# Eight unread products in place of seven in front of the first attention scores of a fused kernel

## The chip, the cores and the metric

The kernel runs on one core of a Trainium2 chip. The metric is device microseconds of one execution. The engines are TensorE (PE; PEld is its weight load), VectorE (DVE), ScalarE (ACT), GpSimd (POOL) and SyncE (SP, which here only issues transfers).

## The reference

Three blocks follow each other on 2 x 768 rows: an attention whose scores are a window of keys plus 24 block summaries (maxima of the keys, means of the values), a gated feed-forward block, and a mixer over rows and channels. Cut to what matters:

```
k_sum = k.reshape(B, H, nb, 32, D).max(axis=3)
v_sum = v.reshape(B, H, nb, 32, D).mean(axis=3)
scores = [where(|i - j| < 16, q @ k.T / 8, -1e9), q @ k_sum.T / 8 + log(32)]
x  = softmax(scores) @ [v, v_sum]
xk = mu_k * x + (1 - mu_k) * x_prev          # x_prev: the row before
xr = mu_r * x + (1 - mu_r) * x_prev
x  = sigmoid(xr @ w_r) * (relu(xk @ w_k) ** 2 @ w_v)
u  = x + (relu(x.T @ w_tok1) @ w_tok2).T
return u + relu(u @ w_ch1) @ w_ch2
```

The weights come as 64-bit floats.

## The kernel before

Attention works on tiles of 128 rows. For the first of the two batches a step is one tile and every second head (`e` 0 or 1); for the second batch both halves go together. In a step, `s_stage` makes 8 or 16 small score products (sp, L367) into one of two score banks per half; VectorE masks and reduces them (L385, four per half), ScalarE takes exponentials (L387), the second batch is normalised on GpSimd (L399), TensorE transposes (pt, L405), a copy brings the result back (PT, L408 or L410), and `v_stage` multiplies with the values (pv, L425). In the first batch `rb` (L441) spreads the normalisers and L445 applies them. The block maxima are ks (L287, VectorE), which GpSimd copies into each key tile (kw, L293, twelve copies per batch: the "key sums" below); the block means are vrs (L309), transposed into vp (L318), copied to vs (L320, ScalarE) and spread by small transfers (L339).

Work of the feed-forward block fills the gaps: `main` multiplies with w_k (ko, L541), squares (`k2_tile`: rl L553 on ScalarE and L554 on VectorE, kh L555 on ScalarE, kl L556 on GpSimd) and multiplies with w_v (acc, L541). Its input is mixed in `mixed` (tmp L530 on GpSimd, xk L531 on VectorE, xh L532, xl L533). Each operand is held as a rounded high part and a low part, so one product is three. A weight block is decoded in `Weights.step`: L153 on ScalarE, L157 and L163 on VectorE into one of two wf buffers, then the high part by L174 on ScalarE and the low part by L175 on GpSimd; L157 of the next but one weight waits until that L175 has freed its buffer. A float32 product is two passes and so two records in the trace; a product of the rounded type is one.

`spin(n)` issues n products of the unit matrix with itself (128 x 512) into the bank of ko. Nobody reads them. `SPIN0` of them stand in front of everything else on TensorE, and one more behind each of the first `SPIN_UNITS` attention steps.

The order on each engine is not written by hand. The program is recorded in the order of the Python code, and a scheduler with a timeline of its own then places the instructions of each engine; `ahead(n)` gives a call a higher priority, `behind` and `after` add an order without a wait on the chip. An instruction of another length early in the program can therefore move others far from it.

Of the kernel before, what the change touches and what calls it, by code (L numbers as in the profile page):

```python
# [28 lines left out]
RATIO, NR, RATIO2 = 1.2, 25, 1.8  # L29
SIDE_EVERY = 3  # L30
AHEAD = 4
SPIN0 = 7
SPIN, SPIN_UNITS = 1, 8
WFIRST = 2
S2COST, S3COST, S4COST = 4, 2, 3
# [22 lines left out]
def fused_kernel(ctx, tc, q, k, v, vt, mu, w_k, w_v, w_r, w_t1, w_t2, w_c1, w_c2, out):  # L58
# [557 lines left out]
    def spin(n):  # L616

        o = bank("ko", 1, [128, 4, 128], "spin")
        for _ in range(n):
            after(nc.tensor.matmul(o, ident, ident.unsqueeze(1).to_broadcast([128, 4, 128]), start=True, stop=True))  # L620


    spin(SPIN0)
    for t in range(NT):
# [515 lines left out]
```

## Time and profile before

| | us |
|---|---|
| three runs | 506.04, 506.87, 511.75 (median 506.87) |
| profiled execution | 506.84 |
| its span, first to last instruction | 504.9 |
| around the span | 1.94 |
| TensorE busy | 489.1 (97%) |
| VectorE, ScalarE, GpSimd busy | 319.6, 239.7, 240.0 |

Times in the trace count from the span's start. The busy time of TensorE is that of products as they follow each other; it tells that TensorE had work, not that it ran at its peak. PEclk is the granted clock as a share of the full 2.4 GHz; 0.50 is the other level, 1.2 GHz.

### The profile page before, as it was taken

What the parts mean: (1) busy time and instruction counts of PE and PEld (TensorE: products, weight loads), DVE (VectorE), ACT (ScalarE), POOL (GpSimd) and SP (SyncE); (2) the same over time, 40 slices, a digit from 0 to 9 for tenths busy, and PEclk for the clock granted to TensorE, in tenths of its full rate; (3) what the DMA queues carried; (4) which work ended last, traced back from release to release, by engine and by line L of the source; (5) the groups of instructions that cost most, each with busy time, mean ns of one, the idle gap of its engine ahead of it and who ended that gap; (6) DMA issues with size and microseconds to landing.
All of it is one profiled execution on the core that took longest, in us unless ns stands there. A gap on an engine that the chain in (4) does not pass through costs nothing.

```text
span 504.9 us, 8793 instructions
## 1 busy us (share of the span) xinstructions
PE 489.1 (97%) x3278; PEld 407.0 (81%) x3278; DVE 319.6 (63%) x638; ACT 239.7 (47%) x541; POOL 240.0 (48%) x294
## 2 busy tenths in 40 slices
PE   7999997999999999999999999999999999999996
PEld 3567785888888898887887787878888999989995
DVE  3888998641514365698789789646479638354352
ACT  1778746872443545655456555554554435011110
POOL 5335587862543457488845535764941813000000
PEclk9899998899999999999999999999999999999999
DMA  8999940321000650000550999629351404163102
GB/s 265 298 294 345 345 124 13 89 80 40 20 1 1 233 186 0 1 0 7 162 167 5 386 398 329 215 91 320 132 167 42 140 30 167 51 201 112 56 1 83
DMA packets 35914, 70.63 MB, mean 140 GB/s; under 512 B 3072, under 2 KB 12288, under 8 KB 35872
## 3 DMA queue, kind: packets, MB, share of 16 engines
q1 hardware_dynamic: 34288, 69.09, 42.1%
q10 hardware_dynamic: 1584, 0.98, 0.7%
q8 instruction: 26, 0.43, 0.4%
q14 instruction: 16, 0.13, 0.1%
HBM read 60.04 MB, written 9.44 MB: 138 GB/s over the span
## 4 chain that ended last, share of the span: by engine, by line
PE 65%; DVE 14%; DMA 11%; ACT 4%; POOL 3%; issue 3%; SPq 1%; DVEq 0%; ACTq 0%; POOLq 0%
PE o L952 12%; PE ko L541 11%; PE m L541 11%; PE acc L541 10%; PE o L980 7%; PE go L541 5%; DMA wst<-in_moe_w_v_dram 4%; PE ro L541 3%; DVE wf L163 3%; DMA wst<-in_moe_w_ch_dram 2%; DMA xT<-in_vt_dram 2%; DVE xk L531 2%; PE pv L425 2%; PE sp L367 2%; DVE xl L533 2%
## 5 line engine op out<-in xcount | busy, mean ns | idle before, releaser
L175 POOL TENSOR_TENSOR w<-wf,w 128x512 fp32r<-128x512 f32 x50 | 69.0, 1387 | 60.8 <-ACT w L174 57.7
L541 PE MATMUL ko<-xh,w 128*128 128x256 f32 x384 | 76.4, 288 | 1.7 <-POOL w L175 0.9
L541 PE MATMUL m<-u,w 128*128 128x256 f32 x504 | 65.1, 283 | 0.7 <-DVE mw L843 0.7
L541 PEld LDWEIGHTS m<-u,w 128*128 128x128 f32 x504 | 63.4, 191 | 2.8 <-DVE mw L843 0.9
L541 PEld LDWEIGHTS ko<-xh,w 128*128 128x128 f32 x384 | 61.2, 188 | 5.4 <-POOL w L175 1.1
L541 PE MATMUL acc<-w,kh 128*128 128x512 f32 x192 | 61.4, 404 | 0.0
L952 PE MATMUL o<-w,gh 128*128 128x512 f32 x192 | 59.1, 391 | 0.0
L541 PE MATMUL ko<-xl,w 128*128 128x256 f32 x192 | 54.4, 283 | 1.1 <-DVE xl L533 1.1
L174 ACT CAST w<-wf 128x512 fp32r<-128x512 f32 x50 | 30.9, 620 | 50.3 <-DVE wf L163 48.5
L163 DVE SCALAR_TENSOR_TENSOR wf<-wst,wf 128x512 int32<-128x512 int32 x50 | 47.5, 958 | 8.8 <-ACT wst L153 7.7
L556 POOL TENSOR_TENSOR kl<-rl,kh 128x512 fp32r<-128x512 f32 x24 | 34.3, 1430 | 36.0 <-ACT kh L555 32.6
L530 POOL TENSOR_SCALAR tmp<-xT,oms 128x256 f32<-128x256 f32 x52 | 38.5, 748 | 21.2 <-DVE xk L531 12.4
L554 DVE TENSOR_TENSOR rl<-rl 128x512 f32<-128x512 f32 x24 | 18.7, 781 | 46.0 <-ACT rl L553 45.8
L387 ACT ACTIVATE pe<-pe,mn 128x120 f32<-128x120 f32 x96 | 36.6, 383 | 14.8 <-DVE mn L385 14.6
L531 DVE SCALAR_TENSOR_TENSOR xk<-xT,mus,tmp 128x256 f32<-128x256 f32 x52 | 39.3, 788 | 5.1 <-POOL tmp L530 4.7
L153 ACT ACTIVATE wst<-wst 128x512 f32<-128x512 f32 x62 | 40.9, 674 | 2.7 <-DMA wst<-in_moe_w_ch_dram 2.7
L541 PEld LDWEIGHTS acc<-w,kh 128*128 128x128 f32 x192 | 35.3, 192 | 7.3 <-ACT pe L387 0.3
L952 PEld LDWEIGHTS o<-w,gh 128*128 128x128 f32 x192 | 34.7, 188 | 6.2
L541 PE MATMUL acc<-w,kl 128*128 128x512 f32 x96 | 37.8, 404 | 0.9 <-POOL kl L556 0.9
L541 PEld LDWEIGHTS ko<-xl,w 128*128 128x128 f32 x192 | 36.2, 188 | 2.2 <-DVE xl L533 1.3
L952 PE MATMUL o<-w,gl 128*128 128x512 f32 x96 | 37.1, 391 | 0.0
L541 PE MATMUL go<-u,w 128*128 128x512 f32 x144 | 35.7, 393 | 0.0
(119 smaller groups left out, 950.9 us busy)
## 6 DMA issues: line engine op xcount, KB each, us to landing
wst<-in_moe_w_ch_dram SPq DMA_DIRECT2D x36, 512.0 KB, 7.3
w<-stored SPq DMA_DIRECT2D x24, 512.0 KB, 5.5
stored<-w SPq DMA_DIRECT2D x24, 256.0 KB, 4.8
wst<-in_moe_w_k_dram SPq DMA_DIRECT2D x8, 512.0 KB, 7.9
wst<-in_moe_w_v_dram SPq DMA_DIRECT2D x8, 512.0 KB, 9.9
wst<-in_moe_w_tok_dram SPq DMA_DIRECT2D x6, 512.0 KB, 4.9
out_dram<-o SPq DMA_DIRECT2D x12, 256.0 KB, 2.3
kw<-in_k_dram SPq DMA_DIRECT2D x9, 320.0 KB, 5.0
```

Source lines behind the costliest of these rows:

```text
L153: a = nc.scalar.activation(top.bitcast(F32), top.bitcast(F32), AF.Prelu, scale=2.0 ** -112, alpha=2.0 ** 32)
L163: nc.vector.scalar_tensor_tensor(wi, top, 3, wi, ALU.logical_shift_left, ALU.bitwise_or)
L174: r = nc.scalar.copy(hi, src)
L175: eng.tensor_tensor(lo, src, hi.bitcast(F32), ALU.subtract)
L387: nc.scalar.activation(pe, pe, AF.Exp, bias=mn[:, p:p + 1], scale=-1.0, accum_out=den[:, p:p + 1])
L530: nc.gpsimd.tensor_scalar(tmp, xT[:, d, x0 - 1:x0 - 1 + MW], om[:, d:d + 1], 1.0, ALU.mult, ALU.mult)
L531: nc.vector.scalar_tensor_tensor(xk[:, d], xT[:, d, x0:x0 + MW], mu[:, d:d + 1], tmp, ALU.mult, ALU.add)
L541: nc.tensor.matmul(o, l, r, start=(first and i == 0), stop=(last and i == 3 * n - 1))
L554: nc.vector.tensor_tensor(rl, rl, rl, ALU.mult)
L556: nc.gpsimd.tensor_tensor(lo, rl, hi.bitcast(F32), ALU.subtract)
L952: nc.tensor.matmul(accs[c][t], l, r, start=(first and j == 0 and i == 0), stop=(last and j == 1 and i == 2))
L980: nc.tensor.matmul(accs[0][t], l, r, start=(k == 0 and i == 0), stop=(k == NF2 - 1 and i == 2))
```

## The change

One constant: the number of products that stand in front of everything else on TensorE.

```
-SPIN0 = 7
+SPIN0 = 8
```

All else follows from the scheduler. The set of instructions is the same but for that product. On TensorE the order differs at two places, between the 73rd and the 95th product and between the 337th and the 561st, of 2834; on VectorE, ScalarE and GpSimd in the same stretches of time, and on SyncE in two query loads (L353) that go behind transfers of vs (L339). After that all engines stand as before.

The start of TensorE, as the difference of the two programs (spin are the unread products, sp the scores):

```order
 L1136 UNCONDITIONAL_BRANCH
-L620 MATMUL spin<-ident 128x512 x7
+L620 MATMUL spin<-ident 128x512 x8
 L367 MATMUL sp<-kw,xT 64x120 x13
 L620 MATMUL spin<-ident 128x512
```

Only the count moved here. VectorE while the key maxima of the second batch are made (ks), before:

```order
L287 TENSOR_REDUCE ks<-kw 128x4x4
L531 SCALAR_TENSOR_TENSOR xk<-xT,mus,tmp 128x256
L163 SCALAR_TENSOR_TENSOR wf<-wst,wf 128x512
L445 TENSOR_TENSOR xT<-xT,rb 128x4x128
L157 TENSOR_SCALAR wf<-wst 128x512
L287 TENSOR_REDUCE ks<-kw 128x4x4
L531 SCALAR_TENSOR_TENSOR xk<-xT,mus,tmp 128x256
L554 TENSOR_TENSOR rl<-rl 128x512
L163 SCALAR_TENSOR_TENSOR wf<-wst,wf 128x512
L309 TENSOR_REDUCE vrs<-ybuf 128x48
L157 TENSOR_SCALAR wf<-wst 128x512
L287 TENSOR_REDUCE ks<-kw 128x4x4 x2
```

and now:

```order
L157 TENSOR_SCALAR wf<-wst 128x512
L287 TENSOR_REDUCE ks<-kw 128x4x4
L157 TENSOR_SCALAR wf<-wst 128x512
L445 TENSOR_TENSOR xT<-xT,rb 128x4x128
L531 SCALAR_TENSOR_TENSOR xk<-xT,mus,tmp 128x256
L163 SCALAR_TENSOR_TENSOR wf<-wst,wf 128x512
L531 SCALAR_TENSOR_TENSOR xk<-xT,mus,tmp 128x256
L163 SCALAR_TENSOR_TENSOR wf<-wst,wf 128x512
L554 TENSOR_TENSOR rl<-rl 128x512
L309 TENSOR_REDUCE vrs<-ybuf 128x48
L287 TENSOR_REDUCE ks<-kw 128x4x4 x2
L157 TENSOR_SCALAR wf<-wst 128x512
```

One weight step (L157) went from ahead of the last two maxima to behind them, and the other L157 and the fourth maximum came up ahead of L445. TensorE around the last scores of the second batch's first pair, before (acc and ko are products of the feed-forward block, vp transposes of the block means):

```order
L541 MATMUL ko<-xh,w 128x256
L541 MATMUL acc<-w,kl 128x512
L541 MATMUL acc<-w,kh 128x512 x2
L541 MATMUL acc<-w,kl 128x512
L318 MATMUL vp<-ident,vrs 24x128 x2
L367 MATMUL sp<-kw,qT 64x120
L541 MATMUL ko<-xh,w 128x256
L541 MATMUL ko<-xl,w 128x256
```

and now:

```order
L318 MATMUL vp<-ident,vrs 24x128 x2
L541 MATMUL acc<-w,kl 128x512 x2
L541 MATMUL acc<-w,kh 128x512 x2
L541 MATMUL acc<-w,kl 128x512
L541 MATMUL acc<-w,kh 128x512 x2
L541 MATMUL acc<-w,kl 128x512
L367 MATMUL sp<-kw,qT 64x120 x4
L541 MATMUL ko<-xh,w 128x256
L541 MATMUL ko<-xl,w 128x256
L367 MATMUL sp<-kw,qT 64x120 x3
L541 MATMUL ko<-xh,w 128x256 x2
```

The acc group that stood ahead of the single last score stands ahead of seven scores now, and the ko products behind or between them. ScalarE at the same place, before (rl empties the bank of ko, the CAST makes a weight's high part, pe are exponentials):

```order
L174 CAST w<-wf 128x512
L153 ACTIVATE wst<-wst 128x512
L553 ACTIVATE rl<-ko 128x512
L174 CAST w<-wf 128x512
L153 ACTIVATE wst<-wst 128x512
L320 ACTIVATE vs<-vp 24x512
L555 CAST kh<-rl 128x512
L387 ACTIVATE pe,den<-pe,mn 128x120 x8
```

and now:

```order
L320 ACTIVATE vs<-vp 24x512
L174 CAST w<-wf 128x512
L153 ACTIVATE wst<-wst 128x512
L387 ACTIVATE pe,den<-pe,mn 128x120 x2
L174 CAST w<-wf 128x512
L553 ACTIVATE rl<-ko 128x512
L153 ACTIVATE wst<-wst 128x512
L387 ACTIVATE pe,den<-pe,mn 128x120 x6
L555 CAST kh<-rl 128x512
```

L553, which stood ahead of a weight's cast, stands behind it and behind two exponentials; L555 (kh) stands behind six more.

## Rows read from the trace of the kernel before

**Rows 1.** The page, part 1: TensorE, busy us, share of the span, instructions.

```profile
PE 489.1 (97%) x3278; PEld 407.0 (81%) x3278; DVE 319.6 (63%) x638; ACT 239.7 (47%) x541; POOL 240.0 (48%) x294
```

**Rows 2.** Busy us (count) by engine in four stretches, then PEclk, DMA share, GB/s.

```profile
40.00:60.00 20.00, 17.93 (x234) 15.12 (x228) 20.00 (x61) 15.72 (x50) 12.97 (x14) 1.00 1.06 360
80.00:92.00 12.00, 8.94 (x56) 6.64 (x57) 11.24 (x47) 8.86 (x35) 9.03 (x12) 0.72 0.22 59
92.00:110.00 18.00, 17.94 (x218) 15.05 (x216) 8.09 (x47) 15.08 (x53) 13.78 (x30) 1.00 0.24 66
110.00:501.00 391.00, 388.01 (x2315) 332.25 (x2313) 235.40 (x364) 167.71 (x310) 173.87 (x162) 1.00 0.36 121
```

**Rows 3.** The chain of waits: start us, us, what.

```profile
36.73 7.66 DMA wst<-in_moe_w_k_dram
```

**Rows 4.** TensorE in order of time, 79 to 92 us (idle before, releaser in brackets).

```profile
79.45 0.41 PE L367 MATMUL sp<-kw,qT 64*64 64x120 f32 x2
80.63 0.39 PE L541 MATMUL ko<-xh,w 128*128 128x256 f32 x1 [0.77 <-ACT rl L553]
...
82.04 0.50 PE L541 MATMUL ko<-xh,w 128*128 128x256 f32 x2 [0.91 <-POOL w L175]
...
85.01 0.63 PE L367 MATMUL sp<-kw,qT 64*64 64x120 f32 x2 [1.52 <-issue]
...
87.57 1.87 PE L367 MATMUL sp<-kw,qT 64*64 64x120 f32 x30
...
91.89 0.40 PE L541 MATMUL acc<-w,kl 128*128 128x512 f32 x1
92.12 0.28 PE L541 MATMUL ko<-xh,w 128*128 128x256 f32 x1
```

**Rows 5.** TensorE in two stretches: length, busy us, PEclk, DMA share, GB/s.

```profile
12.70:15.95 3.25, 3.25 (x23) 0.50 1.06 322
84.30:91.05 6.75, 6.04 (x40) 0.50 0.27 62
```

**Rows 6.** TensorE products and weight loads in order of time, the first 12 us.

```profile
1.46 8.41 PE L620 MATMUL spin<-ident 128*128 128x512 f32 x14 [1.46 <-POOL ident masks.py:199]
...
8.85 0.19 PEld L620 LDWEIGHTS spin<-ident 128*128 128x128 f32 x1 [0.24 <-issue]
...
11.94 1.78 PE L367 MATMUL sp<-kw,xT 64*64 64x120 f32 x26 [2.08 <-POOL kw L293]
```

**Rows 7.** VectorE in order of time, weight steps.

```profile
58.95 1.29 DVE L157 TENSOR_SCALAR wf<-wst 128x512 int32<-128x512 int32 x1
...
66.98 0.48 DVE L157 TENSOR_SCALAR wf<-wst 128x512 int32<-128x512 int32 x1
...
80.78 1.75 DVE L163 SCALAR_TENSOR_TENSOR wf<-wst,wf 128x512 int32<-128x512 int32 x1
```

**Rows 8.** GpSimd in order of time, 68 to 91 us.

```profile
68.74 4.85 POOL L293 TENSOR_SCALAR kw<-ks 128x96 f32<-128x96 f32 x12
73.57 1.26 POOL L556 TENSOR_TENSOR kl<-rl,kh 128x512 fp32r<-128x512 f32 x1
...
79.63 0.96 POOL L530 TENSOR_SCALAR tmp<-xT,oms 128x256 f32<-128x256 f32 x2 [1.86 <-DVE xT L445]
80.56 1.43 POOL L175 TENSOR_TENSOR w<-wf,w 128x512 fp32r<-128x512 f32 x1
...
89.44 1.39 POOL L399 TENSOR_SCALAR pe<-pe,den 128x120 f32<-128x120 f32 x4 [2.61 <-DVE den L396]
```

**Rows 9.** ScalarE in order of time, one exponential.

```profile
85.05 0.38 ACT L387 ACTIVATE pe<-pe,mn 128x120 f32<-128x120 f32 x1
```

**Rows 10.** The queue of SyncE, in order of time.

```profile
84.27 4.87 SPq L339 DMA_DIRECT2D vw<-vs  x5
```

**Rows 11.** VectorE and GpSimd in order of time, 51 to 53 us.

```profile
51.23 0.68 DVE L163 SCALAR_TENSOR_TENSOR wf<-wst,wf 128x512 int32<-128x512 int32 x1
51.39 1.65 POOL L175 TENSOR_TENSOR w<-wf,w 128x512 fp32r<-128x512 f32 x1 [3.98 <-ACT w L174]
```

## Prediction

> **What bounds the kernel now.** I read the page's slices first, then busy time by stage, then the chain of waits of the first 140 us, then each engine in order of time from 56 to 102 us. TensorE carries the span: 489.1 of 504.9 us [rows 1], and from 110 us to its last product at 501 us it stands still for 3.0 us in all (391 less 388.01) [rows 2]. What is won or lost before 110 us therefore reaches the end nearly one for one, because the order of the products after that point is the same in both kernels. Before that two other things rule. Up to about 44 us the chain runs through transfers, weight after weight; its last piece lands at 44.39 [rows 3]. From 40 to 60 us VectorE is busy for 20.00 of 20 us [rows 2]. Between 80 and 92 us TensorE is idle for 3.06 us (12 less 8.94) and its granted clock averages 0.72 [rows 2]: three waits of 0.77, 0.91 and 1.52 us [rows 4], then the low level, 1.2 GHz, a granted clock of 0.50 from about 84.3 to 91.1 us [rows 5]. That is where an order of instructions can gain or lose something.
>
> **The change part by part.**
>
> *The eighth product.* Seven products are 14 passes, 1.46 to 9.87 us; the last passes start 0.43 us apart (0.19 of weight load and 0.24 of waiting) [rows 6]. One more is 2 x 0.43 = 0.86 us, so TensorE comes free at 10.73. The first score starts at 11.94, released by the key sums on GpSimd [rows 6]. Cost: nothing, with 1.21 us of cover left. Without that cover it would be 0.86 us at that place, and even this would lie under the transfers up to 44 us. It adds no wait.
>
> *The clock behind it.* Before, TensorE idles for 2.08 us from 9.87 [rows 6], and from about 12.7 to 16.0 us it runs at the low level [rows 5]. With 1.21 us of idling this fall may not come; then the products of these 3.3 us finish up to 1.7 us sooner. I take that at nothing for the end, since the transfers to 44 us do not depend on it; the bound is 0 to -0.3 us.
>
> *The early order (16 to 36 us).* Five scores are pulled in front of a group of transposes on TensorE, and one copy on ScalarE goes behind two exponentials (2 x 0.38 us). Both lie under the transfers. Taken as nothing, bounds plus and minus 0.3 us, since VectorE still meets the same weights at 44 us.
>
> *Key maxima and key sums (56 to 74 us).* On VectorE the six maxima (ks) of the second batch are moved up, and one weight step (L157, 0.4 of the 0.48 us from 66.98) goes behind the last two. Another L157 took 1.29 us, beside a subtraction on GpSimd, three times as much [rows 7]. In the new order it comes just as that subtraction ends, so about 0.6 us more may be saved. I take 1.0 us (bounds 0.4 and 1.3): the last maximum ends at 67.7 in place of 68.7, and the twelve key sums on GpSimd run from 67.7 to 72.55 in place of 68.74 to 73.57 [rows 8]. The subtraction kl behind them then ends at about 73.8 (72.55 + 1.26).
>
> *TensorE up to the last score of the first pair.* In the old order the sixteenth score product comes at 79.45, after everything else of its group, and ends at 79.86 [rows 4]. In the new order the acc products come before the last scores. They can use kl from 73.8; before them stand nine scores, pv, rb, four acc and two vp, which I work out from the group's start at 71.4: 0.6 + 0.55 + 0.55 + 0.95 + 0.2 = 2.9, to 74.3. Then: eight acc products at 0.234 us (from one start to the next, 91.89 to 92.12 [rows 4]) = 1.9 (76.2), four scores, two ko, three scores = 0.7 (76.9), ten ko of half the columns at 0.117 = 1.2 (78.1). The same work that ended at 79.86 ends at 78.1: 1.75 us ahead.
>
> *The new wait.* The next score needs a bank that VectorE empties with its first four L385 steps, and the next ko needs the bank emptied by ScalarE's relu (L553). Both are queued behind more than before. VectorE: L157 must wait until GpSimd has subtracted w (to 75.5). Then GpSimd makes two tmp of 0.48 [rows 8] and the next w, 76.5 to 77.8; L163 stands beside it and ends at about 78.3 (beside a w it took 1.75, ending 0.5 us after that w [rows 7, 8]). With L531 and L157 it is 79.05; two L385 at 0.20, 79.45; another L163 beside the w of 79.2 to 80.6, ending at 81.1; two L385, 81.5. So the score starts at about 81.6. ScalarE: the cast that waits for that L163, 81.15 to 81.7, then L553 to 82.2; before, L553 stood ahead of that cast and let the ko product start at 80.63 [rows 4]. TensorE is idle from 78.1 to about 82.2 save for one score: 4.0 us in place of 3.2. What is queued behind: twelve ko, thirteen scores, then the acc group.
>
> *From 82.2 us on.* At the full clock twelve ko take 1.4 and thirteen scores 0.85, so 84.5. The four acc products wait for kh on ScalarE: L553 to 82.2, L153 0.6, six exponentials at 0.38 [rows 9] = 2.3, cast 0.5, so 85.6. Then 4 x 0.234, three small products (0.3) and 8 x 0.234 end at 88.8, where the same work ended before at 92.12 [rows 4]: 3.3 us ahead. At the low level from 82.2 to 91.1 instead, at twice 0.234 us for an acc product and 15 scores in 1.87 us [rows 4]: ko 2.8 (85.0), scores 1.6 (86.6), acc 1.9, small ones 0.6 (89.1), four acc products to 91.1, four more at 0.234: 92.0, or 0.1 us ahead. The trace of before has no row for which level this stretch will get. The nearest are the two falls it shows, after 2.08 us of idling and after 3.2 us in pieces, which lasted 3.3 and 6.8 us [rows 5]. Four us of idling speaks for a fall, and an earlier one than before, so also an earlier rise. I take the middle, 1.7 us ahead.
>
> *What else moves.* The normalising on GpSimd (L399), which paces TensorE from 92 to 100 us, starts at 89.44 [rows 8]; in the new order it follows a kl that ends at 86.9, 2.5 us sooner, so it does not take the 1.7 us back. On SyncE the third query load of the batch goes behind the five small copies of vs. Those took 4.87 us [rows 10]; vs is made some 7 us sooner (its two transposes end near 74.3, not 79.5), so that load issues at about 81.5, some 5 us ahead of the scores that need it. Cost nothing; if vs were as late as before (84.3), it would issue at 89.2 and cost about 2 us.
>
> *Sum.* 0 + 0 + 0 - 1.7 = -1.7 us: a span of 503.2 in place of 504.9. Around the span lie 506.84 - 504.9 = 1.94 us, so 505.1 us. The profiled time of before, 506.84, is the median of its runs (506.87) almost exactly; those runs reach from 506.04 to 511.75, so a measurement of this kernel can tell about 1% from no change, and less is "same" here.
>
> **A rule beside the trace.** My sum lets VectorE lose every meeting with GpSimd. The trace has one meeting the other way: L163 began at 51.23 and took its usual 0.68, and the w that began at 51.39 took 1.65 instead of the 1.43 and less of others [rows 8, 11]. The Trainium skill (SBUF — State Buffer, "SBUF: two separate sides") says that the two share a port pair under an exclusive lock, that whichever starts first keeps it for the whole instruction, and that the other fully blocks. By that rule the L163 of 79.45 decides the new wait: 0.25 us sooner, and it goes first.
>
> **The rivals.**
> 1. *VectorE wins that meeting.* If the L163 starts before the w of 79.2, it takes 0.6 in place of 1.65, the L385 steps, the cast, L553 and the ko products come 1.0 us sooner, and the idling falls to about 3 us. For it: the row just named. Against it: by my times GpSimd is ahead by 0.25 us. Time: 505.1 - 1.0 = 504.1; with the clock at its full level throughout also 502.5 (3.3 + 1.0 ahead).
> 2. *The wait takes back all of it.* The low level holds from 82 to 91 us, 0.1 us is left, 506.7; with the key sums gaining only 0.4 it is 507.2. For it: four us of idling in one piece. Against: an earlier fall should bring an earlier rise.
> 3. *Slower.* The low level comes a second time: TensorE waits for the normalised pe between 89 and 100 us, now that it arrives ahead of GpSimd, and falls again. From the rows, a low stretch of 3.3 us costs 1.7 and one of 6.8 costs up to 3.4. On top of rival 2 this is 508.4 to 510.1 us. It decides itself where idling between 89 and 100 us reaches about 2 us. Against: before, TensorE was busy for 17.94 of 18 us from 92 to 110 [rows 2].
> 4. *The eighth product does not do what it says.* If it held up the first scores, they would start later than 11.94; the cover of 1.21 us excludes it, and the transfers would hide 0.86 us anyway: 506.8.
>
> **How the numbers follow.** Forecast (1 to 2.5 us gained) 0.45, rival 1 0.22, rival 2 and 4 together 0.20, rival 3 0.13. The time is the forecast's, 505.1. The range goes from rival 1 at the full clock, 502.5, to the lower end of rival 3, 508.5; what lies outside is a part of rival 1 and most of the upper half of rival 3, and a margin for what the same order after 110 us may add. Faster by over 1% means under 501.8, which needs rival 1 and more: 0.10. Slower by over 1% means over 511.9, beyond rival 3: 0.07. The rest, 0.83, is within 1%.
>
> **What would show it.** In the profile of the changed kernel: 16 passes in the first group, ending near 10.7, and the first score still near 11.9; the key sums starting near 67.7; vp and the last ko before the wait ending near 78.1; one idle stretch of TensorE of 3 to 4 us around 80, ended by L385 or by L553; L399 starting near 87; TensorE then 1 to 3 us ahead at the same product up to the end. Wrong would be: no idle stretch at 80, or two low stretches, or an early order that moves the 44 us at which the weights meet VectorE; also a different wait after 110 us that eats the lead.

## Result and the profile after

The changed kernel takes 510.56 us (median of 8 runs, 507.68 to 512.63); the kernel before, in 8 runs beside it, 505.63 us (503.17 to 511.75). The ratio is 1.0091, with a 95% interval from 1.0063 to 1.0118: slower by 0.9%, some 5 us. I had forecast 505.1 with a range from 502.5 to 508.5, so it came out the other way and 2 us above the range. The profiled execution took 512.0 us with a span of 510.2, so 5.3 us more span than before.

The page of the changed kernel, part 1, and the granted clock in 40 slices of 12.8 us:

```profile
PE 491.1 (96%) x3280; PEld 408.8 (80%) x3280; DVE 321.7 (63%) x638; ACT 240.0 (47%) x541; POOL 239.3 (47%) x294
...
PEclk9979998899999999999999999999999999999999
```

TensorE works 2.0 us more than before [rows 1]. In the row of the clock the third digit is a 7: from 25.5 to 38 us part of the time went by at the low level.

Busy time by engine in five stretches (count in brackets), then PEclk, DMA share, GB/s, after:

```profile
16.00:40.00 24.00, 21.85 (x181) 14.04 (x180) 17.25 (x75) 17.62 (x68) 6.39 (x8) 0.86 1.08 304
25.05:32.25 7.20, 6.97 (x38) 4.52 (x38) 4.59 (x16) 3.35 (x12) 2.30 (x3) 0.53 1.06 319
80.00:92.00 12.00, 8.09 (x51) 6.10 (x49) 10.79 (x31) 8.37 (x26) 7.80 (x9) 0.78 0.31 83
92.00:110.00 18.00, 18.00 (x196) 14.46 (x196) 10.27 (x47) 13.22 (x44) 15.13 (x28) 0.96 0.12 32
110.00:500.00 390.00, 386.80 (x2346) 332.11 (x2346) 236.12 (x381) 172.75 (x331) 176.73 (x168) 1.00 0.36 121
```

The stretch from 16 to 40 us, of which no row was shown, in the kernel before:

```profile
16.00:40.00 24.00, 24.00 (x258) 16.38 (x256) 19.54 (x83) 19.64 (x72) 7.09 (x9) 1.00 1.08 294
```

From 110 us on the two agree (390 less 386.80 is 3.2 us of idling; before it was 3.0 [rows 2]), so all is lost ahead of that. Two places lose it. From 16 to 40 us TensorE had been busy for 24.00 of 24 us at the full clock; now it is idle for 2.15 us, and its clock averages 0.86. From 80 to 92 us it idles for 3.91 us, before 3.06 [rows 2].

The early place, TensorE in order of time (idle before, releaser), after:

```profile
22.56 1.04 PE L367 MATMUL sp<-kw,xT 64*64 64x120 f32 x16
25.28 1.43 PE L367 MATMUL sp<-kw,xT 64*64 64x120 f32 x10 [1.68 <-DMA xT<-in_q_dram]
26.64 2.08 PE L620 MATMUL spin<-ident 128*128 128x512 f32 x2
28.65 0.67 PE L367 MATMUL sp<-kw,xT 64*64 64x120 f32 x4
29.24 1.11 PE L405 MATMUL pt<-ident,pe 128*120 128x128 f32 x4
30.28 2.00 PE L441 MATMUL rb<-ident,dens 128*64 128x128 f32 x16
```

and before:

```profile
23.76 1.04 PE L367 MATMUL sp<-kw,xT 64*64 64x120 f32 x16
24.72 1.13 PE L620 MATMUL spin<-ident 128*128 128x512 f32 x2
25.69 0.60 PE L405 MATMUL pt<-ident,pe 128*120 128x128 f32 x4
26.22 1.09 PE L441 MATMUL rb<-ident,dens 128*64 128x128 f32 x16
27.24 0.62 PE L367 MATMUL sp<-kw,xT 64*64 64x120 f32 x6
```

The first line is the same group of scores in both; after has it 1.2 us earlier, because the fall at 12.7 us [rows 5] does not come. Then the five scores that the new order pulls ahead (25.28; rows count two passes for each score, rb and unread product) wait for 1.68 us for the query load of the fourth tile. Behind them stand the transposes (pt) and the eight rb products, which do not need that load. Before, these went first, and the scores came when the load had landed. Behind the wait the clock falls: one unread product takes 2.08 us, not 1.13, and the row 25.05:32.25 has 0.53. SyncE had issued that load 6.9 us before the scores start (25.28 less 18.41):

```profile
18.41 0.55 SPq L353 DMA_DIRECT2D xT<-in_q_dram  x1
```

The chain of waits of the changed kernel runs through this load, then along TensorE to rb (L441), for which VectorE's L445 waits:

```profile
18.41 6.74 DMA xT<-in_q_dram
25.28 1.43 PE sp L367 x10
...
41.62 0.95 PE rb L441 x15
42.66 0.69 DVE xT L445
```

So TensorE hands its lateness to VectorE. Before, the same L445 waits for rb too (1.80 us, at 39.32), although the chain [rows 3] names a transfer there.

The late place, TensorE after:

```profile
70.61 0.28 PE L318 MATMUL vp<-ident,vrs 128*24 128x128 f32 x1 [0.70 <-DVE vrs L309]
...
75.58 0.83 PE L367 MATMUL sp<-kw,qT 64*64 64x120 f32 x18
...
79.31 0.38 PE L318 MATMUL vp<-ident,vrs 128*24 128x128 f32 x2
...
83.82 0.28 PE L541 MATMUL ko<-xh,w 128*128 128x256 f32 x1
87.87 1.43 PE L367 MATMUL sp<-kw,qT 64*64 64x120 f32 x6 [3.77 <-issue]
...
97.21 0.40 PE L541 MATMUL acc<-w,kl 128*128 128x512 f32 x1
```

All is 3.30 us later than before at the first vp (67.31 there, 70.61 here). Against that, the last product ahead of the wait ends at 84.1 (80.8 in the time of before; 79.86 there [rows 4]), the wait is 3.77 us long, and the acc products that ended at 92.12 end at 97.44.

To follow lateness from run to run I use three places that every kernel has: the group of scores behind the second rb group (39.14 us before), the first vp, and the first pv group of the second batch. What lies between them is not quite the same set of products in the old and the new late order. All from the profiles, start in us:

| profile | scores | first vp | pv | scores to vp | vp to pv | span |
|---|---|---|---|---|---|---|
| before | 39.14 | 67.31 | 100.72 | 28.17 | 33.41 | 504.9 |
| changed | 42.49 | 70.61 | 105.59 | 28.12 | 34.98 | 510.2 |
| changed, again (h3) | 38.79 | 66.92 | 101.50 | 28.13 | 34.58 | 505.7 |
| e1 | 37.73 | 65.90 | 98.33 | 28.17 | 32.43 | 502.7 |
| e2 | 43.77 | 71.87 | 106.86 | 28.10 | 34.99 | 511.5 |
| e3 | 38.07 | 66.18 | 101.13 | 28.11 | 34.95 | 505.7 |
| e4 | 40.21 | 68.39 | 101.06 | 28.18 | 32.67 | 505.6 |
| f1 | 38.22 | 66.55 | 101.68 | 28.33 | 35.13 | 505.5 |
| f2 | 38.68 | 66.81 | 101.38 | 28.13 | 34.57 | 506.8 |
| f3 | 37.92 | 66.03 | 100.05 | 28.11 | 34.02 | 505.5 |
| f4 | 38.10 | 66.27 | 98.53 | 28.17 | 32.26 | 504.2 |
| h1 | 37.73 | 65.86 | 100.48 | 28.13 | 34.62 | 505.8 |
| h2 | 37.94 | 66.04 | 101.55 | 28.10 | 35.51 | 506.8 |
| g1 | 37.53 | 67.23 | 100.78 | 29.70 | 33.55 | 505.0 |
| g2 | 37.49 | 65.45 | 100.96 | 27.96 | 35.51 | 505.9 |
| g3 | 37.09 | 65.23 | 100.00 | 28.14 | 34.77 | 504.2 |
| g4 | 39.66 | 67.06 | 100.53 | 27.40 | 33.47 | 504.9 |

Between scores and vp little changes: what is late at 38 us is as late at 66 us, within 0.4 us, in fifteen of the seventeen. The exceptions are g1, whose queues are mixed (TensorE waits 1.25 us for kh at 66.19), and g4, which makes up 0.77 us, as much as one L163 of VectorE is shorter there: at 40.44, behind a w of GpSimd, it takes 0.68 us, in e1 at 38.51, beside that w, 1.46. From pv to the end lie 403.8 to 405.7 us, so a difference of 1 us in one span is not to be read.

### The profile page after: what moved, and what is told of

Read it like the earlier page. It is cut to its first block, busy times and chain, and to the rows that moved or that the text cites. A ratio compares the mean times of both kernels' runs of the same rounds, so it can differ in the third digit from the quotient of the medians.

```text
span 510.2 us, 8798 instructions
## 1 busy us (share of the span) xinstructions
PE 491.1 (96%) x3280; PEld 408.8 (80%) x3280; DVE 321.7 (63%) x638; ACT 240.0 (47%) x541; POOL 239.3 (47%) x294
## 4 chain that ended last, share of the span: by engine, by line
PE 66%; DVE 14%; DMA 11%; issue 4%; POOL 3%; ACT 2%; SPq 0%; DVEq 0%; POOLq 0%; ACTq 0%
PE o L952 12%; PE ko L541 11%; PE m L541 11%; PE acc L541 10%; PE o L980 6%; PE go L541 5%; DMA wst<-in_moe_w_ch_dram 4%; DVE wf L163 3%; PE sp L367 2%; PE pv L425 2%; PE ro L541 2%; DVE xk L531 2%; PE pt L405 2%; DMA ybuf<-in_v_dram 2%; DMA stored<-w 2%
## 5 line engine op out<-in xcount | busy, mean ns | idle before, releaser
L175 POOL TENSOR_TENSOR w<-wf,w 128x512 fp32r<-128x512 f32 x50 | 68.9, 1384 | 70.0 <-ACT w L174 69.9
L541 PE MATMUL ko<-xh,w 128*128 128x256 f32 x384 | 77.6, 291 | 0.1
L541 PE MATMUL acc<-w,kh 128*128 128x512 f32 x192 | 60.3, 398 | 0.0
L163 DVE SCALAR_TENSOR_TENSOR wf<-wst,wf 128x512 int32<-128x512 int32 x50 | 49.0, 989 | 8.8 <-ACT wst L153 7.9
L530 POOL TENSOR_SCALAR tmp<-xT,oms 128x256 f32<-128x256 f32 x52 | 37.8, 736 | 20.2 <-DVE xk L531 12.8
## 6 DMA issues: line engine op xcount, KB each, us to landing
wst<-in_moe_w_ch_dram SPq DMA_DIRECT2D x36, 512.0 KB, 6.7
w<-stored SPq DMA_DIRECT2D x24, 512.0 KB, 4.1
wst<-in_moe_w_k_dram SPq DMA_DIRECT2D x8, 512.0 KB, 7.5
wst<-in_moe_w_v_dram SPq DMA_DIRECT2D x8, 512.0 KB, 10.2
wst<-in_moe_w_tok_dram SPq DMA_DIRECT2D x6, 512.0 KB, 4.6
```

The costliest lines, as they stand in the source:

```text
L163: nc.vector.scalar_tensor_tensor(wi, top, 3, wi, ALU.logical_shift_left, ALU.bitwise_or)
L175: eng.tensor_tensor(lo, src, hi.bitcast(F32), ALU.subtract)
L530: nc.gpsimd.tensor_scalar(tmp, xT[:, d, x0 - 1:x0 - 1 + MW], om[:, d:d + 1], 1.0, ALU.mult, ALU.mult)
L541: nc.tensor.matmul(o, l, r, start=(first and i == 0), stop=(last and i == 3 * n - 1))
```

## Experiments

The scheduler makes the order, so an edit of one number moves places that have nothing to do with each other. For the experiments the order is written out. A function at the end of the file chains each engine's instructions by edges that fix the issue order and add no wait; its table QUEUES lists the order that the scheduler gave to the kernel before, to the changed kernel, or a splice of the two at about 50 us.

```python
    for engine, text in QUEUES.items():
        ...
            for i in some:
                if last is not None:
                    tc.add_manual_dep(i, last.name, mybir.DependencyInfo(
                        mybir.DependencyClass.NoSync, mybir.DependencyReason.DATA), reason="queue order")
                last = i
```

Theory A: the early order (scores ahead of their load). Theory B: the order from 56 us on. Theory C: the eighth product itself. Ratios are to the kernel before on the same chip, with 95% intervals; its medians there were 505.2 to 505.7 us.

**Product and order apart.** e1 has eight products and the old order, e2 seven and the new order, e3 and e4 eight products and the two splices:

```diff
-SPIN0 = 7
+SPIN0 = 8
...
-    w2.release()
+    in_queue_order(tc, nc); w2.release()
...
+QUEUES = {
+    "PE": (
```

> Eight products in front, but every engine takes all its instructions in the order of the kernel before. Theory A (the early order: five scores on TensorE wait for their query load, with transposes queued behind them): nothing is lost, and the 1.2 us that TensorE is ahead at 24 us may stay, 504.4 to 505.6 us. Theory B (the order from 56 us on loses the time): the same, 505.6. Theory C (the eighth product itself costs the time): about 510.6, as the changed kernel.

e1: 504.98 us, ratio 0.9982 (0.9958 to 1.0007). The eighth product costs nothing, nor does the written order; C falls.

> Seven products in front, every engine in the order of the changed kernel. A: the five scores come up to their query load again, but TensorE arrives later by up to 1.2 us, so the wait is 0.5 to 1.7 us; with the low level behind it 508 to 511 us, without it about 507.5. B: 508 to 511. C: 505.6, as before.

e2: 509.47 us, 1.0074 (1.0044 to 1.0104). The new order alone, without the product, makes 4.1 us of the loss. In its profile, that of the slowest of its runs, the load came at 26.56 us after a wait of 3.29 us, twice the most that I had expected, and the scores of the table are 6 us later than in e1.

> Eight products; the order of before up to about 50 us (TensorE's five scores and ScalarE's one copy), the order of the changed kernel from there on. A: of the 5.3 us, the 3.3 us lost before 70 us come back: 506 to 507.5 us. B: nothing comes back, 510 us. My prediction's own sum for the late part would give 503 to 504.

e3: 506.99 us, 1.0031 (1.0010 to 1.0052).

> Eight products; the order of the changed kernel up to about 50 us, that of before from there on. A: 3.3 us late, 508.5 to 509.5 us. B: 505.6 us. In its profile, A wants a wait of TensorE of about 1.7 us for the query load at 25 us, a low clock behind it, and some 3 us of lateness from there to the end.

e4: 507.64 us, 1.0035 (1.0010 to 1.0060). Both halves lose, each on its own: 2.0 us (e3 less e1) and 2.7 us (e4 less e1), together 4.7 of the 5. A and B each hold for their half; A had wanted 508.5 or more in e4, but in its profile the low level behind the wait lasts from 26 to 29.5 us only. The table says the same by profile: e4 is late at the scores (40.21) and not behind vp (32.67), e3 is late behind vp (34.95) and hardly at the scores.

**What the early half is made of.** f1 is the changed kernel in its own order, with one DMA of SyncE moved up: the query load of the fourth tile is issued right behind that of the third, ahead of five others.

```diff
 SyncE's queue, in QUEUES
-    query 2, mu, w_k 0, w_v 0, v 2a, v 2b, query 3, w_k 1
+    query 2, query 3, mu, w_k 0, w_v 0, v 2a, v 2b, w_k 1
```

> The changed kernel in its own order, save that SyncE issues the query load of the fourth tile six places sooner, ahead of mu and the first two weights. Theory A (five scores wait for that load): TensorE's wait of 1.7 us at 25 us and the low level behind it go, and the time falls from 510.6 to about 507.0 us, what the run with the old early order took. Rival D (the order of the scores and transposes itself costs, or the load was only the last of several late things): 509 to 510.6 us.

f1: 507.48 us, 1.0047 (1.0031 to 1.0064), within 0.5 us of e3. SyncE's queue has both query loads together:

```profile
10.71 1.39 SPq L353 DMA_DIRECT2D xT<-in_q_dram  x2
```

TensorE runs the five scores right behind the sixteen passes ahead of them, now one row of 26:

```profile
22.46 1.75 PE L367 MATMUL sp<-kw,xT 64*64 64x120 f32 x26
```

It has no wait for a query load in this profile, its clock from 25 to 32 us is 1.00, and the scores of the table start at 38.22 (e3: 38.07). With the same order of scores and transposes the early loss is gone, as far as the intervals tell. So the order cost nothing but the wait and what the wait drew after it.

f2 parts these two: three unread products of half the columns in the wait.

```diff
-                b, t, es = steps[i]
+                b, t, es = steps[i]; i == 4 and spin(3, EXTRA)
...
+                extra.append(nc.tensor.matmul(o[:, :w], ident, ident.unsqueeze(1).to_broadcast([128, w, 128]), start=True, stop=True).ins.name); continue
```

> The changed kernel in its own order, with three unread products of 256 columns ahead of the five scores, some 1.5 us of work in the wait for the query load. If the low clock behind the wait carries the larger part of the loss, the wait stays and the level does not fall: 507.0 + 1.7 = 508.7 us or a little less. If the wait alone costs, and the low level nothing: 510.6. If such products do not hold the level: 510.6 too, with a granted clock of 0.50 from 25 us on.

f2: 508.69 us (506.81 to 510.45), 1.0063 (1.0040 to 1.0087). TensorE in the wait:

```profile
22.98 1.56 PE L620 MATMUL spin<-ident 128*128 128x256 f32 x6
24.63 0.80 PE L367 MATMUL sp<-kw,xT 64*64 64x120 f32 x10
```

The scores start as late as ever for their load, the clock stays at 1.00, and the group of the table starts at 38.68: 3.8 us sooner than in the changed kernel, 0.6 later than in e3. The median is as expected, but its interval is wide enough for 507 as well. That the products held the clock is not shown by this one profile: the next run keeps it without them.

h3 is the changed kernel once more.

> The changed kernel itself, for one more profile and beside the others on one chip: 507.5 to 512.5 us. Where the mean granted clock of a run is 0.992 or more, the low level at 25 us should be missing or shorter and the time lie at 507.5 to 508.5; at 0.987, with it, at 510.5 to 512.5 us.

h3: 510.45 us (507.49 to 512.26), 1.0084 (1.0053 to 1.0115). The execution that was profiled took 507.49, with the same wait of 1.66 us and no fall behind it:

```profile
22.05 1.04 PE L367 MATMUL sp<-kw,xT 64*64 64x120 f32 x16
24.75 0.80 PE L367 MATMUL sp<-kw,xT 64*64 64x120 f32 x10 [1.66 <-DMA xT<-in_q_dram]
...
27.46 1.14 PE L441 MATMUL rb<-ident,dens 128*64 128x128 f32 x16
...
38.79 1.31 PE L367 MATMUL sp<-kw,xT 64*64 64x120 f32 x28
```

```profile
25.05:32.25 7.20, 7.20 (x75) 4.78 (x70) 5.19 (x17) 4.14 (x14) 1.78 (x2) 1.00 1.07 317
```

Two profiles of one program: with the low level the scores start at 42.49, without it at 38.79, 3.70 us apart. Of these, 0.51 lie ahead of the wait (the scores at 22.56 and 22.05), so the level takes 3.19. From the same scores (22.34 in e1) to those of the table e1 needs 15.39 us and h3 16.74, so the wait takes 1.35. The granted clock also parts the runs: over both sets, the four of the changed kernel with a mean granted clock of 0.992 or more took 507.5 to 508.1 us, the other twelve (0.986 to 0.990) 509.2 to 512.6. The Trainium skill (TensorE: Matmul & The Clock Gate, Terms) puts the penalty at the time spent throttled, times the share of pulses that the gate takes out; for the 7.2 us at a mean of 0.53 that estimate is 3.4, and this trace agrees within 0.3 us.

**What the late half is made of.** f4 puts six unread products of half the columns into the three waits of [rows 4], in the old order; they are written to the bank of pv, which nothing uses there.

```diff
+            i == n0 and spin(6, EXTRA, "pv")
```

> Eight products, the order of before everywhere (505.0 us), with six unread products of 256 columns in the three waits of TensorE between 78 and 84 us. If idling there brings the low level: no granted clock of 0.50 after 80 us, four products after the waits at 0.23 us in place of 0.5, and 502.5 to 503.5 us, faster than both kernels. If the level falls all the same, or the products run past the waits: 505 to 506 us.

f4: 505.22 us, 0.9998 (0.9982 to 1.0013). The products do what they should, the level does not fall anywhere (80 to 92 us, before: 0.72 [rows 2]):

```profile
80.00:92.00 12.00, 11.59 (x110) 8.56 (x109) 10.53 (x47) 9.34 (x38) 9.03 (x11) 1.00 0.29 72
92.00:98.00 6.00, 5.83 (x58) 4.30 (x57) 4.56 (x23) 5.71 (x23) 6.00 (x14) 1.00 0.24 70
```

and it gains nothing. From vp to pv it is 32.26 against 32.43 us in e1, which has 7 us at the low level there. In the old order that level costs next to nothing. GpSimd, which makes the normalised pe, is busy for 6.00 of 6 us from 92 to 98 us (second row), in e1 too; what TensorE finishes sooner does not get its pe sooner. The chain of waits says the same: in f4 it runs over GpSimd (L399 and L175) from 88.7 to 92.6 us, in e1 over TensorE. By that rule of the Trainium skill (TensorE: Matmul & The Clock Gate, Terms) an estimated 3.4 us (12 us at a mean of 0.72) should have come back; the measurement decides, and it is 0. In all eleven runs of f4 the mean granted clock is 0.998 or more.

h1 does it in the new late order, with seven such products in the wait of 3.8 us, and h2 with four, after f3's mending.

> Eight products, old early order, new late order (507.0 us), with seven unread products of 256 columns, some 3.5 us, in TensorE's wait of 3.8 us at 80 us. In the old late order such products held the clock at its full level and gained nothing. If in the new late order TensorE is the bound behind its wait (it ran there without a pause for 17 us, 7 of them at the low level), holding the level gives 2 to 3 us: 504 to 505 us. If the wait itself, or VectorE and GpSimd, carry the loss: 507 us.

h1: 507.04 us, 1.0027 (1.0006 to 1.0047), as e3. Busy time and clock from 80 to 92 us, then TensorE:

```profile
80.00:92.00 12.00, 9.29 (x70) 6.93 (x70) 11.79 (x48) 9.82 (x38) 7.71 (x10) 1.00 0.30 97
```

```profile
79.19 3.19 PE L621 MATMUL spin<-ident 128*128 128x256 f32 x14
83.14 0.39 PE L367 MATMUL sp<-kw,qT 64*64 64x120 f32 x2 [0.77 <-issue]
...
90.04 0.39 PE L367 MATMUL sp<-kw,qT 64*64 64x120 f32 x2 [1.29 <-issue]
```

A full clock (0.997 or more in all twelve runs), and yet 2.71 us of idling: the score that was reached sooner waits for 1.29 us. Holding the clock alone does not bring the late half back.

f3 moves two places in the queues that stand in the wait: on VectorE the L163 between the first L385 steps goes behind all eight, on ScalarE the relu L553 ahead of the cast that waits for that L163.

```diff
 VectorE's queue
-    L385 L385 L163 L385 L385 L385 L385 L385 L385
+    L385 L385 L385 L385 L385 L385 L385 L385 L163
 ScalarE's queue
-    L387 L387 L174 L553 L153 L387 L387 L387 L387 L387 L387
+    L387 L387 L387 L553 L387 L387 L387 L174 L153 L387 L387
```

> Eight products, old early order, new late order (507.0 us), but on VectorE the L163 that stands between the first L385 steps goes behind all eight, and on ScalarE the relu L553 goes ahead of the cast that waits for that L163. If these two queue places make the wait of 3.8 us: TensorE waits about 2 us at 80 us, and the time is 505.0 to 506 us. If the wait is set by what VectorE does before 80 us, or GpSimd takes over: 507 us.

f3: 506.94 us, 1.0025 (1.0010 to 1.0040). The wait is cut as expected:

```profile
81.56 1.43 PE L367 MATMUL sp<-kw,qT 64*64 64x120 f32 x6 [2.05 <-issue]
```

In the profile that is worth 0.93 us from vp to pv (34.02 for 34.95 in e3); in the medians 0.05, nothing that can be told from zero. The rival holds: it is not these two places alone.

> The same with the two queue places on VectorE and ScalarE mended, which made the wait 2.05 us, and four unread products of 256 columns in it. If the low level is what is left of the late loss: 503.5 to 504.5 us, at or below the kernel before. If not: 507 us.

h2: 508.26 us, 1.0045 (1.0026 to 1.0063). Its profile has a full clock up to 89.5 us (0.51 from there to 93) and new waits, 0.84 us for the cast kh and 1.26 us for a score. A shorter wait and the full clock up to there give nothing either.

> Eight products, old early order, new late order on VectorE, ScalarE, GpSimd and SyncE, but TensorE in its old order throughout. If TensorE's own late order (the second ko block behind the acc products and the scores, so that ko products no longer lie behind the short waits) loses the 2 us: 505 to 505.5 us. If what the other engines do in the new order loses it: 507 us or more, with TensorE waiting about 3.8 us or longer near 80 us all the same.

> The other half: TensorE alone in the new late order, the other engines in the old order. If TensorE's own order loses the time: 507 us. If the other engines' order does: 505 to 505.5 us.

g1: 508.87 us, 1.0058 (1.0034 to 1.0081). g2: 508.00 us, 1.0052 (1.0032 to 1.0071). Either half of the new late order is worse beside the old other half than both are together (e3, 506.99). Taken together, neither theory wanted that. The longest wait of TensorE, in g1 and in g2:

```profile
84.80 0.58 PE L541 MATMUL ko<-xh,w 128*128 128x256 f32 x1 [4.43 <-ACT rl L553]
```

```profile
83.34 1.43 PE L367 MATMUL sp<-kw,qT 64*64 64x120 f32 x6 [4.40 <-issue]
```

A queue pays by what it meets in the others: the two mixtures wait 4.4 us.

> Eight products, old early order, new late order, but GpSimd in its old order. My prediction had the key sums 1 us sooner; in the changed kernel they started 0.6 us later against the same transposes, behind a kl that now stands ahead of them. If that place costs: 506 us or less, key sums about 1 us sooner. If it is off the path: 507 us.

g3: 507.45 us, 1.0037 (1.0017 to 1.0057). The key sums did not come sooner but later, 3.3 us behind the first vp (68.51 less 65.23) against 2.0 in e3, so this does not test what it was made for; that the time stays within 0.5 us of e3 speaks for their place being off the path.

**A faster kernel?** TensorE is busy throughout from 16 to 40 us, and three of the unread products that follow the attention steps lie there. g4 leaves these three out, in the old order, and issues the last three query loads sooner.

```diff
-                if i < SPIN_UNITS:
+                if i < SPIN_UNITS and i not in (4, 5, 6):
```

> Eight products in front, old order, without the three unread products that follow the attention steps 5, 6 and 7 (1.07 us each, between 23 and 32 us, where TensorE is busy without a pause), and with the query loads of the last three tiles three to six places sooner on SyncE. If TensorE sets the pace from 16 to 40 us, as the early loss says, the scores at 38 us come 2 to 3 us sooner, and 502 to 503 us at the end, faster than both kernels. If the transfers to 44 us set it (my prediction), or VectorE from 40 to 60 us: no change, 505 us. If the level falls without these products: 506 to 508 us.

g4: 505.97 us, 1.0010 (0.9990 to 1.0030). TensorE:

```profile
32.48 1.47 PE L425 MATMUL pv<-PT,ybuf 120*64 120x64 f32 x16 [1.62 <-issue]
...
39.66 1.39 PE L367 MATMUL sp<-kw,xT 64*64 64x120 f32 x28
```

At 29.82 us it is 2.5 us ahead of e1, which has this group of scores at 32.28. Then it waits for 1.62 us, the level falls (0.50 from 33 to 39.5 us), and the scores of the table start at 39.66, 1.9 us later than in e1. In this profile the three products would have paid for themselves by holding the level; its runs without them reach from 504.16 to 507.84. No version is faster than the kernel before by more than the measurement tells; e1 is the nearest.

## Why the prediction was wrong, step by step

**The early order (16 to 36 us)** failed, and with it the forecast: "Both lie under the transfers. Taken as nothing, bounds plus and minus 0.3 us." I had read from the chain [rows 3] that transfers rule up to 44 us, and gave TensorE slack it did not have. That chain's transfers are weights, to be decoded on ScalarE and VectorE; TensorE was busy for 24.00 of 24 us, VectorE's L445 waits for its rb, and from 38 to 66 us its lateness passes on (28.0 to 28.3 us in fifteen of seventeen profiles). And I moved five scores without asking when their operand lands. The load has no slack: the old order reaches it about when it lands (e3 even waits for 0.62 us there). Measured: 2.7 us by the medians; by the profiles of the changed kernel 1.35 for the wait and 3.19 for the level, where it falls.

**The eighth product** was right: first scores at 11.78, e1 as fast as before. **The clock behind it** was right in kind (no fall at 12.7 us). That it is worth nothing at the end rested on the same error: by profile the lead of 1.2 us reaches the scores of the table in the old order (37.73 in e1 against 39.14). The runs do not tell it from zero, since e1's median is only 0.4 us below.

**Key maxima and key sums** was wrong. In the time of before (less 3.30) the last maximum ends at 68.4, 0.2 us sooner and not 1.0, and the sums start at 69.3 (72.62), not at 67.7, because w and kl hold GpSimd up to then:

```profile
71.35 1.29 POOL L556 TENSOR_TENSOR kl<-rl,kh 128x512 fp32r<-128x512 f32 x1
72.62 4.65 POOL L293 TENSOR_SCALAR kw<-ks 128x96 f32<-128x96 f32 x12
...
82.29 1.45 POOL L175 TENSOR_TENSOR w<-wf,w 128x512 fp32r<-128x512 f32 x1
...
85.56 1.26 POOL L175 TENSOR_TENSOR w<-wf,w 128x512 fp32r<-128x512 f32 x1
```

**TensorE up to the last score of the first pair**: forecast 78.1, measured 80.8 (84.10 less 3.30), so 0.9 us behind the old order, not 1.75 ahead. The group starts 0.9 us later than I had it (75.58 less 3.30 is 72.28, not 71.4): four acc products that stood ahead of the first vp stand behind it now. From there to its end lie 8.5 us, not 6.7: I had put pv, rb, scores and ko too low. Of the 3.7 us by which the late half missed (acc ends at 97.44 less 3.30, that is 94.1, for 90.4) 2.7 lie here, the rest behind the wait.

**The new wait** was right in place, cause and size: 3.77 us for 4.0, but it ends some 2.4 us later than forecast (84.57; I had the score at 81.6 and the next ko at 82.2). The fourth L385 ends it, behind the two L163 (rows of VectorE below):

```profile
87.49 0.27 DVE L385 CUSTOM_DVE_ANT_0 pe<-sp,mask 128x120 f32<-128x120 f32 x1
```

**From 82.2 us on**: I took the middle of 88.8 and 92.0. It took 9.57 us from the end of the wait (87.87) to the end of acc (97.44), at the low level up to about 93 us, where the low case had 9.8. But h1 has a full clock and needs 9.2 (83.14 to 92.33): I had left out that the next pair's scores wait for VectorE again. Rival 2, the wait that takes back all, comes nearest for this half, but it ends 2 us behind (e3 less e1), not level. Rival 3 had the right sign and a second low stretch, but at 89 to 100 us; it came at 25.

**What else moves** was half right. L399 starts at 90.6 (93.94 less 3.30), 1.2 us later than before and not 2.5 sooner: the kl ahead of it waits 2.55 us for kh. The query load issues at 82.7 (86.00 less 3.30), not at 81.5. Neither shows as idling of TensorE: it is busy for 18.00 of 18 us from 92 to 110.

**Rival 1** asked who is first where L163 meets the w on GpSimd (rows of GpSimd above). VectorE:

```profile
82.51 1.77 DVE L163 SCALAR_TENSOR_TENSOR wf<-wst,wf 128x512 int32<-128x512 int32 x1
...
85.57 1.79 DVE L163 SCALAR_TENSOR_TENSOR wf<-wst,wf 128x512 int32<-128x512 int32 x1
```

GpSimd starts 0.22 us and at most 0.01 us ahead (82.29 and 85.56), and L163 takes 1.77 and 1.79 us, so VectorE did not win and rival 1 did not come. The rule of the Trainium skill (SBUF — State Buffer, "SBUF: two separate sides") that I had weighed agrees with the first; the second is too close to call.

Left open is which link carries the late 2 us. Shown is what it is not by itself: the product (e1), the clock (h1), the two queue places in the wait (f3), TensorE's queue (g1). The queues of VectorE, ScalarE and SyncE were not put back one by one. There are 277 passes from vp to pv, first in e1, then in e3:

```profile
65.90:98.33 32.43, 30.16 (x277) 24.14 (x275) 27.39 (x86) 20.95 (x70) 27.47 (x44) 0.89 0.15 45
```

```profile
66.18:101.13 34.95, 31.05 (x277) 24.63 (x278) 29.55 (x85) 21.50 (x70) 28.33 (x46) 0.90 0.14 41
```

Of the 2.52 us between them 1.63 are more idling (3.90 less 2.27) and 0.89 more busy time. The mean clock is the same, so the passes are not slower on the whole; the new order has four acc passes more and three ko passes fewer in there, some 0.6 us at 0.234 and 0.117 each.

The traces say where it goes. The score that VectorE holds back starts no later in the new order: 17.26 us behind the first vp (87.87 less 70.61), before 17.70 (85.01 [rows 4] less 67.31). But from it to pv lie 17.72 us, before 15.71 (e3 and e1: 17.70 and 14.76). Twelve ko products that the old order makes ahead of this score, between its short waits, stand behind it in the new one, and they take 2.9 us there, at the low level. In h1, at the full clock, they take 1.6, and TensorE then waits for kh and for the next score. That these twelve carry the late 2 us is read from the traces and not tested: no run puts them back ahead of the score, in the otherwise new order, together with the L553 that they wait for.

## What to carry to other kernels

A chain of waits that runs through transfers gives no slack to an engine that is busy throughout the same stretch; look at its busy share there, and at who waits for it, before you call a reordering free. Where a reordering pulls an instruction forward on an in-order queue, find its last operand's landing time, and count what stands behind it. What the low level behind a wait costs depends on whether TensorE is the bound there: in this kernel 3.2 us at 25 us, and nothing at 84 us in the old order (f4). Look also at which products fill a wait for another engine: moved behind it they cost time, as the traces of the late half suggest.

## What the hardware showed unasked

The same wait does not always bring the low level: after 1.68 us of idling it fell in one execution of the changed kernel, after 1.66 us in another it did not. The granted clocks of its sixteen runs fit this as a large part of their scatter; only two of them have a profile. And it can fall after little: in e1 it falls from 80.5 to 87.5 us behind two waits of 0.74 and 0.93 us.
